# Third batch in groups of 256 rows, with seven half-size products for its second feed-forward product

## The chip, the cores and the metric

The kernel runs on one core of a Trainium2 chip. The metric is the device time of one execution in microseconds (us), and a time given for a kernel is the median of its runs. The engines are TensorE (PE; its weight loads are shown apart as PEld), VectorE (DVE), ScalarE (ACT), GpSimd (POOL) and SyncE (SP, which issues most DMAs).

## What is computed

Two layers, one after the other. The first is a linear attention with a decaying state, over 4 batches, 8 heads, 768 steps and 64 dimensions:

```
state = gamma[h] * state + k_t v_t^T          # per head, 64 x 64
y_t   = q_t @ state / sqrt(64)
```

Its output, as x of 4 x 768 x 512, goes through a Fourier mix and a feed-forward layer:

```
X   = fft(fft(x, axis=1), axis=2)
u   = x + real(X)
un  = (u - mean(u)) / sqrt(var(u) + 1e-6)      # over the 512 columns
out = u + max(un @ w_ch1, 0) @ w_ch2           # w_ch1 512 x 2048, w_ch2 2048 x 512
```

## The kernel before

The kernel works batch by batch (0 to 3). For each batch it runs the attention in four pairs of heads, in chunks of 128 steps; then the Fourier mix, written as matmuls against cosine and sine tables after the input has been folded by its symmetries; then, by blocks of 128 rows, the norm; then the feed-forward layer. Attention and Fourier mix of one batch are interleaved with the feed-forward layer of the batch before, so that TensorE always has matmuls to do.

The order of work is written out by hand as a list of units, in the string `LATER` (its third part, behind the second bar, holds nearly all of it). Every unit issues a few instructions on one to three engines, and `held` pins each instruction behind the one before it on its own engine, so that the list fixes the order on every engine; an engine that waits holds all that stands behind it. Units are named by kind and digits, the first digit being the batch. The names used below:

- `i`, `h`: feed-forward up product of batch 0 by blocks of 128 rows, and of a batch by groups of 384 rows (`h_unit`: 4 matmuls of 384 columns for one of 16 feature blocks, then the relu on ScalarE, `@a`, or VectorE, `@v`). The result lies in the tile `ht16`.
- `c`, `O`: down product (`ch_unit`: for 128 rows, 16 matmuls of 512 columns, four in a unit) and `rows_out`, which scales it, adds u and stores the rows.
- `H`, `j`, `p`, `q`, `w`: the same layer in groups of 256 rows, which batch 3 already uses. `hp_unit` does feature blocks n and n + 8 for 256 rows (8 matmuls of 256 columns; `@s` is two relus on ScalarE, `@b` one on each engine). The down product of a group is then a 2 x 2 block product (features in two halves, output columns in two halves, rows in two blocks of 128), done with seven products instead of eight: `sum_unit` (`j`) forms sums and differences of blocks of the relu's result on VectorE, `wsum_unit` (`w`) those of the weights, `p_unit` does one of seven products (8 matmuls of 256 columns), and `add_unit` (`q`) adds a product to u or to an output row.
- `s`, `a`, `y`: attention (state, masked scores, output; the copy of `y` into x is on ScalarE). `cq`, `ck`, `cv`: casts on GpSimd of the loaded q, k and v; `lq`, `lk`, `lv`, `l`: the loads; `t`, `tq`, `tk`: transposes on TensorE or by DMA.
- `fs`, `fd`, `fe`, `g`: folds of x on VectorE; `f`: first transform; `gr`: mirrored copies; `x`: second transform; `X`: GpSimd adds x to u; `n`, `u`: statistics and normalised rows; `U`: their transpose (`@d` by DMA).

What is loaded lands in a pool of input tiles (`inp`, eleven buffers), which rotate. Down products, up products and the seven products share three PSUM buffers (`ps_pm`).

Of the kernel before, what the change touches and what calls it, by code (L numbers as in the profile page):

```python
# [12 lines left out]
ALU = mybir.AluOpType  # L13
f32 = mybir.dt.float32
# [5 lines left out]
P = 128  # L20
B, H, S, D = 4, 8, 768, 64
DM = 512
# [30 lines left out]
i02 U01@v x03 U02@a cq11 pz11 i12 x04 X03 x05 i13 X04 l10 n03 i10 l11 l12 i22 i11 cq10 i20 X05  # L53
ck10 l13 i23 n04 i03 i21 u04 n05 c0000 c0001 c0002 cv10 u05 u03 Z r00 ck11 c0003 TB cv11 t10
cq12 c0020 c0021 s100 s101 O00 t11 c0022 cv12 a102 U05@a c0023 a100 ck12 a101 s110 s111 a110
c0010 U03@a c0011 a112 a111 y100 c0012 U04@v s120 y101 y110 cq13 ck13 t12 cv13 s121 c0013 pz00
h014@a y111 t13 O02 O01 h012@a h01F@a pz01 a120 a122 h018@a a121 h01D@a a132 a130 a131 s130 s131
h01E@a y120 lq20 y121 h013@a h01C@a lk20 h015@a lv20 lq21 y130 lk21 y131 ck21 fs10 fd10 h01B@a
h010@a h011@a cq20 h019@a lv21 lq22 fs11 ck20 fd11 lk22 lv22 lq23 g10 tq20 h016@a fe10 h017@a
tk20 fe11 c0100 h01A@v f100@v f110@a lk23 f101@v gr11@v tk21 f111@a c0120 g112 x11 X11 x10 r01  # L60
X10 n11 gr13@v x12 X12 c0101 pz10 cv21 n10 u10 gr10@a c0121 u11 c0102 c0103 c0110 c0111 gr12@v
c0112 cq21 c0113 tq21 O03 c0122 lv23 ck22 n12 u12 O04 U12@v cv20 lq30 s210 U11@a U10@v a202 cv22
c0123 s211 x13 h10E@a r10 tk22 a200 a201 h101@a h105@a s200 cq22 h106@a s201 h102@a ck23 a212
h10F@a O05 a210 s220 h10A@v y200 y201 tq22 cv23 X13 tk23 cq23 h100@a a211 x14 X14 s221 h104@v
h103@a y210 y211 tq23 h10C@a lk30 n14 n13 s230 lv30 h107@a x15 X15 h108@a h10B@a h109@a c1000
a220 c1001 c1002 lq31 cq30 n15 u13 a221 a231 a222 ck30 s231 u15 U15@d a230 u14 U14@d h10D@a tk30
c1010 a232 y221 y220 fs20 c1003 U13@d lk31 c1011 lv31 O10 fd20 y230 y231 fs21 g20 c1020 c1012
c1021 c1022 h116@a c1023 c1013 fd21 cq31 fe20 f200@a fe21 tq30 O12 h112@v lq32 lk32 lv32 f210@v
lq33 h111@a cv31 cv30 h11F@a gr20@a f201@v h118@v gr21@a f211@v g212 h115@a h113@a O11 a302
h11E@v x20 h114@v x22 ck31 X20 tq31 h110@a s300 s301 X22 n20 tk31 ck32 gr23@v x21 X21 h11C@a  # L70
h11B@a lk33 cv32 lv33 h119@a h11A@a s310 h117@a s311 n21 c1110 n22 c1100 c1101 c1102 h11D@a
c1111 gr22@v u22 x23 a300 U22@d a301 u20 U20@d a311 x25 c1112 c1103 X25 ck33 a310 u21 r11 a312
c1113 U21@d O14 c1120 cq33 O13 y300 w11 cq32 c1121 c1122 c1123 O15 h20A@v w21 x24 h200@a h20E@v
y301 X23 h20D@v tq32 h209@v h207@a h20C@v tk32 cv33 r20 tk33 h201@v n23 s330 h20F@a s331 y310
y311 s320 h20B@a h208@v u23 h202@a s321 X24 n24 h203@v h206@a h204@v a320 a322 u24 h205@a tq33
c2010 c2020 a321 c2021 U23@d a330 y320 U24@d y321 n25 a331 u25 c2011 U25@d a332 c2022 c2012 y330
fs30 c2023 fd30 c2013 O21 O22 y331 fs31 g30 fd31 fe31 c2000 h210@a c2001 c2002 h21A@a h217@v
c2003 fe30 h21C@a f311@v h21B@v O20 h212@v f300@v f310@a h218@a gr30@v f301@a gr31@a h213@a
h219@a g312 h216@v x31 x30 X30 h214@a h211@v r21 h21F@a h21D@v x32 h215@v X31 c2100 h21E@a c2120
n31 c2101 c2102 w41 u31 U31@d c2110 n30 w10 w20 w40 u30 U30@d gr32@v c2121 c2122 c2123 O25 c2103  # L80
c2111 O23 w31 H304@v c2112 c2113 O24 gr33@a X32 x33 X33 H300@s w30 n32 H302@a H303@a H301@a
j30104 j30204 u32 H305@b j30304 n33 H306@s H307@b j30148 j30248 U32@d r30 j30404 p301 q301 p304
p305 q305 j30448 j30348 u33 U33@d p302 q302 p306 q306 x35 X35 p303 p307 H313@s q307 n35 q303 x34
H317@b H312@s H310@a H314@v H311@b j31104 j31204 u35 U35@d X34 H316@s n34 H315@s j31148 p311
p314 j31248 j31448 p315 r31 q311 q315 p312 j31404 p316 j31304 q316 j31348 u34 U34@d q312 p313
q313 p317 q317 H325@v H320@v H326@a H323@b H324@a j32136 j32336 H321@v H322@b H327@s j32236
j32103 j32168 p321 p324 j32203 p322 j32368 j32268 r32 q321 j32436 j32303 q322 p326 p325 j32403
q326 p327 q325 j32468 p323 q327 q323
# [7 lines left out]
def kernel(  # L96
# [13 lines left out]
    def pool(name, bufs, **kw):  # L110
# [3 lines left out]
    inp = pool("inp", 11)  # L114
# [12 lines left out]
    obp = pool("obp", 3)  # L127
# [21 lines left out]
        "p (n w) -> p n w", n=4)  # L149
    pmask = const.tile([P, 4], f32, tag="pmask")  # L150
# [64 lines left out]
    def in_tile(name, b):  # L215
        return inp.tile([P, 2, NCH, D], f32, tag="in32", name=f"{name}32")
# [4 lines left out]
    def load_unit(b, i, after=None, names="qkv"):  # L221
        def run():
            h0 = 2 * PAIR_ORDER[i]
            for name in names:
# [3 lines left out]
                t = in_tile(name, b)  # L228
# [12 lines left out]
    def first_load(name, i, eng):  # L241
        def run():
            h0 = 2 * ORD0[i]
            t = in_of[name, 0, i] = in_tile(name, 0)
# [887 lines left out]

# [274 lines left out]
```

## Time and profile before

| | us |
|---|---|
| median of 3 runs | 241.01 (240.26 to 241.2) |
| the profiled execution | 240.78 |
| its span, first to last instruction | 238.4 |
| TensorE busy | 225.2 (94%) |
| VectorE busy | 193.1 (81%) |
| ScalarE busy | 125.0 (52%) |
| GpSimd busy | 83.8 (35%) |

The mean granted clock of TensorE is 0.997 of its full speed. Busy time is the share of the span in which an engine has an instruction in it; matmuls are pipelined, and their ends are modelled, so the time that one costs is read from the distance to the start of the next. In rows of the timeline the columns are start, time, engine, source line, operation, tiles, shapes and count, and in brackets the idle time before and what ended it. In rows of groups the columns behind the count are busy time, mean of one in ns, and idle time before with what ended it. In rows of stretches they are the stretch, then busy time (and number of instructions) of TensorE, its weight loads, VectorE, ScalarE and GpSimd, then granted clock, DMA share and GB/s.

### The profile page before, as it was taken

To read this page: it belongs to the slowest core of one execution; us is meant where nothing else is said; L and a number is where in the kernel's file an instruction comes from. 1 tells how busy PE (TensorE), PEld (TensorE's weight loads), DVE (VectorE), ACT (ScalarE), POOL (GpSimd) and SP (SyncE) were. 2 spreads that over 40 slices of the span, in tenths; PEclk is the share of its full clock that TensorE was granted. 3 is DMA by queue.
4 is the path that set the end of the run, shared out by engine and by line. 5 is a ranking of instruction groups with operands and counts; after the bars stand their busy time and mean duration, and the time that the engine had idled before them with its cause. 6 is when DMAs were issued, how large, how long until landed. Compare 5 with 4: busy or idle time off the path is not lost.

```text
span 238.4 us, 5552 instructions
## 1 busy us (share of the span) xinstructions
PE 225.2 (94%) x2135; PEld 155.6 (65%) x2135; DVE 193.1 (81%) x459; ACT 125.0 (52%) x284; POOL 83.8 (35%) x148
## 2 busy tenths in 40 slices
PE   0888999999999999999999999999999999999993
PEld 0366769856776746766576565655576468898893
DVE  8799984978879798988978879877968768869584
ACT  5989759386788345584245253533245307153220
POOL 8378902554600697553144529200005002120000
PEclk9999999999999999999999999999999999999998
DMA  7999999999999999999799983840210222122202
GB/s 169 237 268 238 234 206 207 207 247 264 196 236 204 224 198 210 218 225 219 157 251 215 213 120 133 160 85 22 88 47 0 44 91 67 25 88 45 91 0 88
DMA packets 101225, 37.18 MB, mean 156 GB/s; under 512 B 91472, under 2 KB 98256, under 8 KB 101200
## 3 DMA queue, kind: packets, MB, share of 16 engines
q1 hardware_dynamic: 96976, 32.65, 66.3%
q0 software_dynamic: 4224, 4.19, 10.7%
q8 instruction: 16, 0.26, 0.5%
q14 instruction: 9, 0.07, 0.1%
HBM read 27.66 MB, written 6.29 MB: 142 GB/s over the span
## 4 chain that ended last, share of the span: by engine, by line
PE 78%; DVE 8%; ACT 5%; DMA 3%; POOL 2%; SPq 1%; issue 1%; DVEq 0%; ACTq 0%
PE psc L1129 24%; PE psh L1094 21%; PE psh L1165 9%; PE ps L1216 7%; PE wkA L678 3%; DMA v<-in_v_dram 3%; PE ps L850 3%; PE wkY L721 2%; PE pq L1004 2%; PE wkY L718 1%; DVE ht L1084 1%; PE wkK L697 1%; ACT qTz L649 1%; SPq L246 1%; PE ps L831 1%
## 5 line engine op out<-in xcount | busy, mean ns | idle before, releaser
L1129 PE MATMUL psc<-w,ht 128*128 128x512 f16 x288 | 67.7, 379 | 0.0
L1087 ACT ACTIVATE ht<-psh 128x384 f16<-128x384 f32 (+2 forms) x89 | 41.7, 481 | 42.5 <-PE psh L1094 25.0
L1094 PE MATMUL psh<-unT,w 128*128 128x384 f16 x320 | 59.7, 326 | 0.1
L1129 PEld LDWEIGHTS <-ht 128*128 128x128 f16 x288 | 27.4, 98 | 27.4
L1037 POOL TENSOR_TENSOR u<-u,x 128x256 f32<-128x256 f32 x21 | 13.4, 636 | 81.9 <-DVE u L1011 71.2
L1094 PEld LDWEIGHTS <-w 128*128 128x128 f16 x320 | 29.9, 98 | 17.1 <-issue 0.3
L1084 DVE TENSOR_SCALAR ht<-psh 128x384 f16<-128x384 f32 (+2 forms) x40 | 22.5, 568 | 6.3 <-ACT ht L1087 2.3
L680 DVE TENSOR_TENSOR atm<-wkA,maskp 128x512 f16<-128x512 f32 x36 | 23.3, 682 | 4.9 <-PE wkA L678 4.8
L466 POOL TENSOR_SCALAR kd<-k,gexp 128x384 f16<-128x384 f32 x24 | 13.9, 592 | 23.4 <-DMA k<-in_k_dram 20.8
L1165 PE MATMUL psh<-unT,w 128*128 128x256 f16 x192 | 21.8, 273 | 0.0
L1165 PEld LDWEIGHTS <-w 128*128 128x128 f16 x192 | 18.7, 98 | 2.3
L1053 ACT ACTIVATE un<-u,stats 128x512 f16<-128x512 f32 x21 | 14.8, 718 | 8.9 <-DVE stats L1049 8.2
L728 ACT ACTIVATE x<-wkY,gexp 128x384 f16<-128x384 f32 x24 | 13.0, 585 | 12.1 <-PE wkY L721 12.1
L704 DVE SCALAR_TENSOR_TENSOR s<-s,gk,wkK 128x128 f16<-128x128 f16 x48 | 16.5, 345 | 3.5 <-ACT s L702 1.8
L1119 DVE SCALAR_TENSOR_TENSOR ob<-psc,stats,u 128x512 f32<-128x512 f32 x18 | 13.1, 739 | 5.0 <-PE psc L1129 4.9
L1006 ACT COPY qn<-pq 128x128 f32<-128x128 f32 x18 | 5.1, 283 | 19.8 <-PE pq L1004 17.0
L1216 PEld LDWEIGHTS <-ht 128*128 128x128 f16 x152 | 14.1, 98 | 1.8 <-ACT ht L1087 0.2
L475 POOL TENSOR_SCALAR v<-v 128x768 f16<-128x768 f32 x12 | 10.0, 840 | 13.0 <-DMA v<-in_v_dram 13.0
L1048 DVE BATCH_NORM_STATS2 bst<-u 128x6 f32<-128x512 f32 x21 | 14.3, 681 | 0.1
L1039 POOL TENSOR_TENSOR u<-u,x 128x256 f32<-128x256 f32 x21 | 14.2, 678 | 0.0
L678 PE MATMUL wkA<-qTz,kT 128*128 128x256 f16 x72 | 11.7, 272 | 0.0
L1107 PE MATMUL psh<-unT,w 128*128 128x128 f16 x192 | 11.6, 219 | 0.1
(190 smaller groups left out, 389.4 us busy)
## 6 DMA issues: line engine op xcount, KB each, us to landing
q<-in_q_dram SPq DMA_DIRECT2D x17, 384.0 KB, 6.2
k<-in_k_dram SPq DMA_DIRECT2D x16, 384.0 KB, 5.6
v<-in_v_dram SPq DMA_DIRECT2D x16, 384.0 KB, 6.5
out_dram<-ob SPq DMA_DIRECT2D x23, 256.0 KB, 2.6
w<-in_moe_w_ch_dram POOLq DMA_DIRECT2D x8, 512.0 KB, 11.4
unT<-un SPq DMA_TRANSPOSE x15, 2.5
kT<-kd SPq DMA_TRANSPOSE x10, 3.1
qTz<-q16z SPq DMA_TRANSPOSE x8, 3.9
```

Source lines behind the costliest of these rows:

```text
L678: nc.tensor.matmul(wk[:, c2], st["kT"][:, c, :], st["qT"][:, :, c, :], start=True, stop=True)
L680: nc.vector.tensor_tensor(out=st["atm"][:, 2 * part:2 * part + 2], in0=wk, in1=maskp[:, PAIR_ORDER[i]].unsqueeze(1).to_broadcast([P, 2, 2, ...
L704: nc.vector.scalar_tensor_tensor(out=s16[:, c], in0=s16[:, c - 1], scalar=gk2[:, hp:hp + 1], in1=wk[:, c - c0], op0=ALU.mult, op1=ALU.add)
L1039: nc.gpsimd.tensor_tensor(out=u[:, kb, 256:512], in0=u[:, kb, 256:512], in1=x[:, kb, 1, 257:1:-1], op=ALU.add)
L1048: nc.vector.bn_stats(bst, u[:, kb, :])
L1053: nc.scalar.activation(un, u[:, kb, :], AF.Identity, bias=stats[:, kb, 0:1], scale=-1.0)
L1084: nc.vector.tensor_scalar(out=dst, in0=src, scalar1=-1.0, scalar2=0.0, op0=ALU.mult, op1=ALU.max)
L1087: nc.scalar.activation(dst, src, AF.Relu, bias=0.0, scale=-1.0)
L1094: nc.tensor.matmul(psh, w116[:, cb, fb * P:(fb + 1) * P], unT[:, cb, rt * 384:(rt + 1) * 384], start=(cb == 0), stop=(cb == 3))
L1129: nc.tensor.matmul(psc_of[b, rb], ht16[:, fb, rb3 * P:(rb3 + 1) * P], w216[:, fb, :], start=(fb == 0), stop=(fb == NFB - 1))
L1165: nc.tensor.matmul(psh[:, t], w116[:, cb, fb * P:(fb + 1) * P], unT[:, cb, g * 256:(g + 1) * 256], start=(cb == 0), stop=(cb == 3))
L1216: nc.tensor.matmul(dst, lhsT, rhs[:, c0:c1], start=(n == 0 and (name is not None or k == 5 and m == 1)), stop=(n == 7), skip_group_check=True)
```

## The change

Batch 2 now does its feed-forward layer as batch 3 does: three groups of 256 rows, each with eight `H` units, twelve `j` units (each sum in three parts: feature blocks 0 to 3, 4 to 6 and 7), seven `p` and six `q` units, in place of 32 `h`, 24 `c` and six `O` units. Its `rstd` units go by two blocks instead of three.

The weights' sums are therefore needed a batch sooner, at a time when all input tiles are in use. So their places are fixed: the first sum lies in the tables `cd16` and `sd16`, which nothing reads after the half tables are made; the other three lie in a new constant tile `wide` of the size of four input tiles. Until batch 2's loads are used up, `wide` serves as four of the eleven input buffers (a load whose turn modulo eleven is 7 or more goes there), and the pool itself shrinks from eleven buffers to seven, which are all that batch 3's loads have. The fourth sum of the relu's result gets a tile `s4` of its own. The pool of output rows shrinks from three buffers to two. A unit `C` (`cg_unit`) is added that the list doesn't use.

The third part of `LATER` is a new list, from batch 0's last units on: other engines for some relus and copies, other places for loads and attention, and another order of the last products (it ends with `p326 q322 q325 j32468 p323 q326 p327 q323 q327`, where it was `q322 p326 p325 j32403 q326 p327 q325 j32468 p323 q327 q323`). The diff, with the middle of the list cut to its part for batch 2:

```diff
@@ the list, new (part) @@
+i02 U01@v i03 x03 X03 U02@a x04 X04 i10 i13 i11 l10 x05 X05 i12 cq10 c0010 n04 i22 l11 c0011
...
+u22 c1113 O14 c1122 a312 w40 c1123 U22@d a311 X25 O15 n25 H202@s s300 ck33 s301 H204@s H203@a
+u23 a300 s311 H201@a a310 H200@a j20104 H207@a j20178 y300 w31 H205@s y301 w30 tk32 j20204
+j20404 cq33 H206@s j20147 j20347 r20 j20378 y310 U23@d tk33 j20278 y311 p201 p204 lv33 cv33 tq32
+q201 j20247 j20304 j20447 tq33 p202 q202 p206 p205 q206 p207 u25 n24 q205 u24 j20478 q207 s320
+s330 r21 s321 H217@a j21178 a320 p203 q203 j21278 U24@d a322 a321 a331 H213@s H210@s s331 j21478
+H212@a H211@a j21104 j21304 j21204 j21378 a332 H215@a H214@s j21404 H216@a a330 y321 j21147
+j21347 p211 j21247 q211 j21447 y320 fs30 y331 y330 p214 p216 fs31 q216 fd31 p215 q215 U25@d p217
+g30 fd30 fe30 fe31 p212 p213 q212 f300@a f301@a q217 f310@v f311@a q213 H221@a g312 x31 gr30@v
+X31 x30 X30 n31 n30 H226@a H222@s H223@a H220@a j22104 j22204 u31 x32 H224@b H225@s H227@b r22
...
@@ pools @@
-    inp = pool("inp", 11)
+    inp = pool("inp", 7)
...
-    obp = pool("obp", 3)
+    obp = pool("obp", 2)
...
+    s4t = const.tile([P, 8, P], f16, tag="s4")
@@ input tiles @@
-    def in_tile(name, b):
+    wide = const.tile([P, 4, 2, NCH, D], f32, tag="wide")
+    early = [(n, 0, i) for n, i in LOADS0] + [("q", 1, 0), ("q", 1, 1)]
+    turns = early + [x for b in (1, 2) for i in range(4) for x in [(n, b, i) for n in "qkv"]
+                     if x not in early]
+
+    def in_tile(name, b, i):
+        n = turns.index((name, b, i)) % 11 if b < 3 else 0
+        if n >= 7:
+            return wide[:, n - 7]
         return inp.tile([P, 2, NCH, D], f32, tag="in32", name=f"{name}32")
@@ sums of weights @@
-    def spare(n, name):
-        t = inp.tile([P, 2, NCH, D], f32, tag="in32", name=name)
-        return t.rearrange("p h c d -> p (h c d)").bitcast(f16)[:, 0:n]
+    tw = wide.rearrange("p s h c d -> p (s h c d)").bitcast(f16).rearrange(
+        "p (k n m) -> p k n m", k=3, n=8)
+
+    def t_of(k, part):
+        if k == 1:
+            return (cd16, sd16)[part].rearrange("p a b -> p (a b)").rearrange(
+                "p (n m) -> p n m", n=4)
+        return tw[:, k - 2, 4 * part:4 * part + 4]
...
-            t = seven["t", k, part] = spare(4 * 256, "wsum").rearrange("p (n m) -> p n m", n=4)
...
-            in1 = half_of(w216, *b, n0, n1) if b else seven["t", k // 2, part]
-            nc.vector.tensor_tensor(out=t, in0=half_of(w216, *a, n0, n1), in1=in1,
+            in1 = half_of(w216, *b, n0, n1) if b else t_of(k // 2, part)
+            nc.vector.tensor_tensor(out=t_of(k, part), in0=half_of(w216, *a, n0, n1), in1=in1,
                                     op=ALU.subtract)
...
@@ units @@
-    ... r=lambda b, g: rstd_unit(b, g, 3 if b < B - 1 else 2), c=ch_unit,
+    ... r=lambda b, g: rstd_unit(b, g, 3 if b < 2 else 2), c=ch_unit, C=cg_unit,
```

More of the change, by code (lines that the diff above doesn't have):

```diff
@@ L52 @@
 |
[L53 to L64, printed above, removed]
@@ L71 @@
[L71 to L82, printed above, removed]
@@ new lines @@
+c0012 n05 TB Z u04 i21 c0013 u05 U05@a r00 n03 c0000 c0001 l12 l13 ck10 t10 cv10 i23 ck11 pz01
+c0002 s100 s101 c0003 cq11 O00 a101 cq12 u03 O01 cv11 i20 U03@a a100 t11 c0020 a102 ck12 U04@v
+cv12 c0021 s110 c0022 s111 y100 y101 h015@v t12 pz00 a111 cq13 a110 h013@a lq20 a112 s120 h011@a
+s121 h01B@v h012@v ck13 cv13 s130 s131 y110 y111 t13 lk20 lv20 lq21 c0023 a120 a122 h01E@a
+h010@a a121 a132 ck20 h018@a a131 y121 y120 O02 pz10 a130 h014@a lk21 lv21 h01C@a h016@a y131
+fs10 lq22 lk22 lv22 y130 fs11 fd10 r01 h01D@a fd11 h01A@a tk20 h017@a h019@a c0100 c0101 cq20
@@ L89 @@
+p322 j32336 p324 p325 q321 j32268 p326 q322 q325 j32468 p323 q326 p327 q323 q327
 """
@@ L1131, in ch_unit, with cg_unit, run @@
         return run
+    def cg_unit(b, g, t, part):
+        def run():
+            rb = 2 * g + t
+            if part == 0:
+                psc_of[b, rb] = ps_pm.tile([P, DM], f32, tag="pm", name="psc")
+            for fb in range(4 * part, 4 * part + 4):
+                nc.tensor.matmul(psc_of[b, rb], hg[:, fb % 8, fb // 8, t * P:(t + 1) * P],
+                                 w216[:, fb, :], start=(fb == 0), stop=(fb == NFB - 1))
+        return run
     seven = {}
@@ L1176, in run @@
         def run():
-            if "s4" not in seven:
-                seven["s4"] = spare(8 * P, "s4").rearrange("p (n k) -> p n k", n=8)
             a11, a12 = hg[:, n0:n1, 0, 0:P], hg[:, n0:n1, 1, 0:P]
@@ L1341 @@
     later = dict(
[L1342 removed]
+        pz=pad_unit,         i=h0_unit, r=lambda b, g: rstd_unit(b, g, 3 if b < 2 else 2), c=ch_unit, C=cg_unit,
         O=lambda b, rb: lambda: rows_out(b, rb), X=add_x_unit, cq=cq_unit, ck=ck_unit,
```

44 lines of the change are left out of this document (26 added, 18 removed).

## The prediction

> **What bounds the kernel now.** I read the page first (busy time, then the chain that ended last), then the busy time of each engine by stretches, then TensorE's own timeline, where the pitch of a matmul is the distance from one row's start to the next row's start.
>
> ```profile
> PE 225.2 (94%) x2135; PEld 155.6 (65%) x2135; DVE 193.1 (81%) x459; ACT 125.0 (52%) x284; POOL 83.8 (35%) x148
> PE 78%; DVE 8%; ACT 5%; DMA 3%; POOL 2%; SPq 1%; issue 1%; DVEq 0%; ACTq 0%
> ```
>
> ```profile
> 40.00:60.00 20.00, 19.20 (x218) 14.02 (x216) 17.43 (x46) 12.74 (x22) 10.41 (x16) 1.00 1.17 236
> 60.00:80.00 20.00, 19.90 (x221) 14.05 (x218) 17.41 (x39) 14.70 (x30) 4.77 (x9) 1.00 1.10 213
> 80.00:100.00 20.00, 20.00 (x174) 12.60 (x173) 17.19 (x44) 10.29 (x29) 14.64 (x26) 1.00 1.21 220
> 146.60:192.75 46.15, 46.15 (x358) 27.62 (x356) 36.80 (x81) 19.43 (x44) 7.28 (x12) 1.00 0.27 63
> ```
>
> TensorE is the bound: it carries 78% of the chain, and from 80 us (the third row) to the tail every stretch of 20 us shows it busy throughout. The fourth row is the stretch that the change rewrites, from the last down product of batch 1 to the first unit of batch 3's feed-forward: TensorE 46.15 of 46.15 us at clock 1.00, VectorE 36.80 (80%), ScalarE 42%. The first two rows hold the only waits worth naming, 0.8 and 0.1 us. So the time of this kernel is the sum of its matmuls plus the places where a list of units leaves TensorE waiting, and I price the change in these two terms.
>
> **The matmuls.** Pitches come from these rows.
>
> ```profile
> 179.99 2.76 PE L1094 MATMUL psh<-unT,w 128*128 128x384 f16 x16
> 182.59 0.39 PE L1004 MATMUL pq<-gk,g 128*128 128x129 f16 x4
> 184.98 7.93 PE L1129 MATMUL psc<-w,ht 128*128 128x512 f16 x36
> 192.75 1.04 PE L1165 MATMUL psh<-unT,w 128*128 128x256 f16 x8
> 202.57 1.91 PE L1216 MATMUL ps<-wsum,ht 128*128 128x256 f16 x16
> 204.32 1.04 PE L1216 MATMUL ps<-w,ht 128*128 128x256 f16 x8
> ```
>
> 384 columns: 2.60 us / 16 = 162.5 ns. 512 columns: 7.77 / 36 = 215.8 ns. 256 columns: 1.75 / 16 = 109.4 ns. Batch 2 now has 2 x 16 x 4 = 128 up matmuls of 384 columns (20.80 us) and 6 x 16 = 96 down matmuls of 512 (20.72). After, it has 3 x 8 x 8 = 192 up matmuls of 256 (21.00) and 3 x 7 x 8 = 168 down products of 256 (18.38). Sum: 39.38 for 41.52, so **-2.1 us**. Everything else on TensorE keeps its count.
>
> The Trainium skill would have this otherwise. "TensorE: Matmul & The Clock Gate", section "Back-to-back issue gap", says that in a stream of weight loads and matmuls the spacing is set by both, and gives about 81 ns at 128 moving columns and 131 at 512; drawn straight between them (an estimate from that page) 384 columns cost 114 and 256 cost 98, and the change would add 35.3 - 27.2 = 8.1 us. The three pitches above do not agree with those figures, and the measurement decides; the mechanism returns as a rival.
>
> **VectorE.** These groups carry its new work.
>
> ```profile
> L1185 DVE TENSOR_TENSOR ht<-ht 128x512 f16<-128x512 f16 x12 | 5.0, 420 | 1.3 <-ACT ht L1087 1.1
> L1185 DVE TENSOR_TENSOR ht<-ht 128x384 f16<-128x384 f16 x6 | 2.0, 353 | 0.7 <-ACT ht L1087 0.7
> L1230 DVE SCALAR_TENSOR_TENSOR u<-ps,stats,u 128x256 f32<-128x256 f32 x6 | 2.9, 483 | 0.5 <-PE ps L1216 0.3
> L1230 DVE SCALAR_TENSOR_TENSOR ob<-ps,stats,u 128x512 f32<-128x512 f32 x3 | 2.3, 751 | 0.7 <-PE ps L1216 0.6
> L1119 DVE SCALAR_TENSOR_TENSOR ob<-psc,stats,u x18: 630/746/752, 55.5 to 195.6; 128x512 f32<-128x512 f32 x18
> L1084 DVE TENSOR_SCALAR ht<-psh 128x384 f16<-128x384 f32 x23 | 12.6, 552 | 1.9 <-PE psh L1094 1.6
> L1153 DVE TENSOR_TENSOR wsum<-w x4: 674/680/954, 144.6 to 197.1; 128x1024 f16<-128x1024 f16 x4
> ```
>
> Added: 36 sums, a third each of four, three and one blocks (420, 353, and some 200 ns for one block, which no row shows: bounds 100 and 353), 12 x 0.97 = 11.7 us; 18 adds, 12 x 0.483 + 6 x 0.751 = 10.3. Gone: 6 row adds of 0.746 (4.4) and the 16 relus that VectorE did for h2 (16 x 0.552 = 8.8), since the new H2 units carry @a or @s (ScalarE) but for two @b. Six weight sums lay in the quoted stretch and four of them leave it (-2.9; 0.7 us each between 100 and 145 us, behind batch 1's products; by the third row VectorE has 14% free thereabouts, so I cost them at nothing; without that cover 8 x 0.7). Some 3 us more of batch 3's attention now fall into it. At full means the old stretch sums to 42.3 us, of which 36.80 are busy time, since successive instructions overlap: a factor of 0.87. The new one sums to 50.8, so 44 us busy for about 47.7 us of matmuls. VectorE goes from 80% to 92%: not the bound, but without room to catch up. ScalarE, 42% busy in the old stretch, takes over the relus with room left.
>
> **The place where that shows** is the fold of batch 3, where the old order has rows for each step:
>
> ```profile
> 167.12 0.34 PE L721 MATMUL wkY<-v,atm 128*128 128x64 f16 x6
> 167.50 0.58 ACT L728 ACTIVATE x<-wkY,gexp 128x384 f16<-128x384 f32 x1 [1.47 <-PE wkY L721]
> 168.50 1.02 DVE L747 TENSOR_TENSOR xab<-x 128x768 f16<-128x768 f16 x2
> 169.56 0.17 DVE L874 TENSOR_TENSOR xg<-xab 128x6 f16<-128x6 f16 x1
> 169.90 1.02 DVE L774 TENSOR_TENSOR eo<-xab 128x768 f16<-128x768 f16 x2
> 170.96 0.57 DVE L788 TENSOR_TENSOR ee<-eo 128x768 f16<-128x768 f16 x1
> 172.51 0.56 DVE L788 TENSOR_TENSOR ee<-eo 128x768 f16<-128x768 f16 x1
> 173.57 0.18 DVE L793 COPY ee<-eo 128x6 f16<-128x6 f16 x1
> ```
>
> By starts, fs costs 1.06 us, g30 0.34, fd 1.06, and fe30 with its copy 1.24. The old list had all of c200x and a dozen h21x as filler. The new one reads y320 fs30 y331 y330 p214 p216 fs31 q216 fd31 p215 q215 p217 g30 fd30 fe30 fe31 p212 p213 ... f300. Count from the moment T at which TensorE has issued y330. TensorE then has six products before f300: 6 x 8 x 0.1094 = 5.25 us. VectorE starts fs30 at about T + 0.3, after y320's copy and the last sums, and ends it at T + 1.35; the copy of y330, last of three at some 0.5 each, is done by T + 1.1. Then fs31 1.06, q216 0.48, fd31 1.06, q215 0.75, g30 0.34, fd30 1.06, fe30 1.24: 6.0 us, so f300 may start at T + 7.3, or some tenths sooner with overlap. TensorE waits for 7.3 - 5.25 = 2.1; with 0.2 for the overlap I take **+1.9 us** (bounds 1.6 and 2.6, the latter if VectorE comes late). q216, q215 and g30 stand in that queue without being needed there. Afterwards f310 finds fe31 done within 0.1 us, H221 and g312 cover the copies, and the first H30 unit stands 22 us behind y330 while its chain (product, add, statistics, norm, transpose) needs some 20: nothing more.
>
> **Early waits.** The new list differs from batch 1's first units on.
>
> ```profile
> 52.73 0.50 PE L644 MATMUL tq<-ident,q16z 128*128 128x128 f16 x6
> 53.95 0.51 PE L644 MATMUL tq<-ident,kd 128*128 128x128 f16 x6 [0.73 <-ACT s L702]
> 54.30 1.03 PE L1129 MATMUL psc<-w,ht 128*128 128x512 f16 x4
> 52.64 1.26 POOL L466 TENSOR_SCALAR kd<-k,gexp 128x384 f16<-128x384 f32 x2 [2.77 <-DMA k<-in_k_dram]
> 63.66 0.83 POOL L475 TENSOR_SCALAR v<-v 128x768 f16<-128x768 f32 x1
> out_dram<-ob SPq DMA_DIRECT2D x23, 256.0 KB, 2.6
> ```
>
> t11 waited there until GpSimd's ck11 had ended at 53.9 (the label names ScalarE; the time fits ck11): its first half took 1.22 us from row to row, the second 0.35, so 0.9 was lost. In the new list t11 stands 19.5 us of matmuls behind i02 instead of 16.8, and the loads, which start behind i13, come 0.45 later: that wait goes, **-0.9**. In turn s130 moves up from 31.7 to 28.6, which is 64.5 on this clock (i02 being at 52.73 - 16.8 = 35.9), while cv13 ended at 64.49 and now ends 0.45 later: **+0.4**. The smaller pool of input tiles costs nothing: for batches 0 to 2 the rotation over eleven is the same, and batch 3's twelve loads find casts that ended well before. The two output buffers (three before) come free 2.6 us after a store is issued, and the next is needed later than that each time.
>
> **The end.** Rows of the old end:
>
> ```profile
> 233.93 1.01 DVE L1230 SCALAR_TENSOR_TENSOR ob<-ps,stats,u 128x512 f32<-128x512 f32 x2 [0.25 <-PE ps L1216]
> 234.17 0.61 PE L1216 MATMUL ps7e<-w,s 128*128 128x128 f16 x8
> 235.13 0.88 SPq L1262 DMA_DIRECT2D out_dram<-ob  x2
> DMA to landing us min/median/max: 1.7/1.8/1.9
> DMA to landing us min/median/max: 2.0/2.0/3.0
> ```
>
> It ended with p323, whose row leaves in two small stores; the second is issued at 235.6 and lands 1.7 later, 2.7 after the last matmul was issued (234.6). The new list ends with p327: 0.2 to the add, 0.75 for it, then the full store with 2.0: 3.0, so **+0.3**. Waits of the new list that I did not find: 0 to 1.5, by the 0.9 of the old one's worst 40 us; I take 0.2.
>
> **Sum:** -2.1 + 1.9 - 0.9 + 0.4 + 0.3 + 0.2 = -0.2 us on the profiled execution's own 240.78 (span 238.4), which stands 0.2 below the median of 241.01. Against that median: **240.8 us**. I treat 0.5% (1.2 us) as what a measurement of this kernel can tell from no change.
>
> **Rivals.**
> *The fold is covered.* If VectorE is ahead of my count, or its steps overlap more, f300 finds its data; then -2.1 stands nearly alone: about 238.6. For it: the old list left TensorE no wait over 0.3 us after 80 us, by an order just as tight. Against: the six products are 5.25 us, and even with nothing in between, fs31, fd31, fd30 and fe30 are 4.4 us behind a copy that ends at T + 1.1. 0.28.
> *VectorE becomes the bound,* from the first H2 unit to the first H3 unit. Price: its 50.8 us at full means, without the overlap, plus some 2 us of waits for GpSimd's additions, would be 52.8 for 47.7 of matmuls: 5.1 us in place of the fold's 1.9, about 244.0. It decides once VectorE's idle share there falls below some 5%. For it: 92% already. Against: the factor of 0.87 in the old stretch. 0.20.
> *The shared read port.* L1153's rows run from 674 to 954 ns: something holds a two-input VectorE instruction for 0.28 us at times. If that is GpSimd, the added sums and the weight sums, now among GpSimd's casts, meet it more often: five meetings in the full stretch are 1.4 us, about 242.2. The Trainium skill, "SBUF — State Buffer", section "Who interferes with whom", has this rule: VectorE with two SBUF inputs and GpSimd exclude each other for a whole instruction. Other two-input rows (L774, 546 to 559) did not show it. 0.06.
> *Weight loads show.* There are 136 more pairs of load and matmul; if a load of 98 ns were not hidden, +13.3 us: 252. The 109.4 ns pitch with a load in each speaks against it. 0.01.
> *The change does not do what it says:* the order is pinned on every engine, so this would be sums or buffers put elsewhere, with the time as it was: 0.03.
>
> ```profile
> L774 DVE TENSOR_TENSOR eo<-xab x12: 546/552/559, 72.9 to 170.4; 128x768 f16<-128x768 f16 x12
> L1216 PEld LDWEIGHTS <-ht 128*128 128x128 f16 x152 | 14.1, 98 | 1.8 <-ACT ht L1087 0.2
> ```
>
> **How the numbers follow.** My forecast has 0.42, with a range of its own from 239.6 to 242.0. Faster by over 0.5%: the covered fold and a little of the forecast's edge, 0.31. Slower: VectorE's bound, the port, the loads and the other edge, 0.31. Within: 0.38. The range takes in the covered fold and stops short of the middle of VectorE's case: 238.5 to 243.2.
>
> **What would show it.** TensorE's rows of batch 2: 192 + 168 matmuls of 256 columns at 109 ns. A gap of about 2 us in TensorE ahead of f300 (L850 of batch 3), ended by VectorE's fold (L790 or L793). No wait ahead of t11's second half, a short one ahead of s130. VectorE at 90 to 94% between H202 and H300. No gap at f300, or several of them at sums and adds, would prove me wrong.

## Result and profile after

The changed kernel takes **237.68 us** (median of 4 runs, 237.33 to 238.87) beside 241.1 for the kernel before (4 runs, 240.26 to 241.88): a ratio of 0.987, interval 0.982 to 0.992. Taken a second time with more runs of the kernel before, it was 237.46 (5 runs) for 240.32, ratio 0.988 [0.986, 0.990]. It is faster by some 3 us, where the prediction had 240.8 and a range from 238.5 to 243.2. The profiled execution took 237.73 us, its span 235.7.

The page of the changed kernel, the engines' busy time and the chain:

```profile
PE 223.2 (95%) x2271; PEld 168.9 (72%) x2271; DVE 197.0 (84%) x490; ACT 133.3 (57%) x304; POOL 83.6 (35%) x148
PE 84%; DVE 5%; SPq 5%; DMA 3%; POOL 1%; issue 1%; ACT 0%; POOLq 0%; DVEq 0%
```

TensorE is still the bound, with 84% of the chain for 78%, and its busy time is 2.0 us less. Next the stretches. The first three rows are the changed kernel's (the prediction's stretch; the same units where they now lie, from H202 to H300; the early part), the fourth is the kernel before in the stretch of the third, the fifth is the changed kernel's just ahead of f300:

```profile
146.60:192.75 46.15, 45.46 (x506) 40.86 (x505) 42.57 (x116) 25.43 (x61) 6.72 (x11) 1.00 0.37 80
144.00:191.60 47.60, 46.91 (x519) 42.13 (x517) 43.84 (x119) 26.93 (x65) 6.81 (x11) 1.00 0.42 84
33.00:60.00 27.00, 27.00 (x341) 21.14 (x339) 21.70 (x56) 18.81 (x39) 12.80 (x19) 1.00 1.18 225
```

```profile
33.00:60.00 27.00, 26.06 (x316) 20.02 (x314) 21.31 (x55) 18.28 (x38) 10.41 (x16) 1.00 1.19 229
```

```profile
164.60:175.10 10.50, 9.82 (x122) 8.66 (x120) 10.22 (x26) 3.85 (x8) 0.00 (x0) 1.00 0.05 11
```

VectorE is busy for 42.57 of 46.15 us, 92% (43.84 of 47.60 where the units now lie, also 92%), and in the last 10 us ahead of f300 for 97%; TensorE loses 0.69 us there. From 33 to 60 us TensorE had idled 0.94 us and now does not idle at all.

The matmuls of batch 2, from TensorE's timeline of the changed kernel (24 up matmuls, then p214 and p216, then the row that follows):

```profile
163.99 2.78 PE L1193 MATMUL psh<-unT,w 128*128 128x256 f16 x24
166.61 0.38 PE L689 MATMUL wkA<-qTz,kT 128*128 128x256 f16 x2
...
168.98 1.91 PE L1242 MATMUL ps<-wide,ht 128*128 128x256 f16 x16
170.73 0.60 PE L1242 MATMUL ps<-cd,ht 128*128 128x256 f16 x4
```

2.62 us / 24 and 1.75 / 16 are 109 ns each, with a weight load for every one.

The place of the forecast, f300. First VectorE's timeline of the changed kernel from fs30 on, then TensorE's (p217, p212, p213, f300):

```profile
169.22 1.97 DVE L758 TENSOR_TENSOR xab<-x 128x780 f16<-128x780 f16 x4
171.11 0.48 DVE L1256 SCALAR_TENSOR_TENSOR u<-ps,stats,u 128x256 f32<-128x256 f32 x1
171.51 1.01 DVE L785 TENSOR_TENSOR eo<-xab 128x768 f16<-128x768 f16 x2
172.44 0.74 DVE L1256 SCALAR_TENSOR_TENSOR u<-ps,stats,u 128x512 f32<-128x512 f32 x1
173.10 0.16 DVE L885 TENSOR_TENSOR xg<-xab 128x6 f16<-128x6 f16 x1
173.30 0.23 DVE L888 TENSOR_SCALAR xg<-xg,sgn 128x6 f16<-128x6 f16 x1
173.43 1.02 DVE L785 TENSOR_TENSOR eo<-xab 128x768 f16<-128x768 f16 x2
174.49 0.57 DVE L799 TENSOR_TENSOR ee<-eo 128x768 f16<-128x768 f16 x1
```

```profile
171.64 1.03 PE L1242 MATMUL ps<-wide,ht 128*128 128x256 f16 x8
172.51 1.04 PE L1242 MATMUL ps<-w,ht 128*128 128x256 f16 x8
173.39 1.04 PE L1242 MATMUL ps<-w,s4t 128*128 128x256 f16 x8
175.11 1.38 PE L861 MATMUL ps<-csp,ee 128*128 128x193 f16 x12 [0.69 <-DVE ee L799]
```

p213 starts at 173.39, and eight matmuls at 109 ns end at 174.26; f300 starts at 175.11. So it waits 0.85 (the 0.69 in the bracket counts from the modelled end), released by the first of fe30's three instructions, L799. Another 0.16 stands ahead of f301.

The early part, from TensorE's timeline: the kernel before, batch 0's up product and the row that follows; then the changed kernel: up units in the same place, t11 (both halves and what follows) and, in the last two rows, an up unit and s130; then GpSimd's cv13 in the changed kernel.

```profile
39.14 7.62 PE L1107 MATMUL psh<-unT,w 128*128 128x128 f16 x128
46.60 3.62 PE L1129 MATMUL psc<-w,ht 128*128 128x512 f16 x16
```

```profile
40.70 0.38 PE L1031 MATMUL pq<-cd,g16r 128*128 128x257 f16 x2
...
41.13 1.06 PE L1118 MATMUL psh<-unT,w 128*128 128x128 f16 x16
42.03 1.03 PE L1140 MATMUL psc<-w,ht 128*128 128x512 f16 x4
...
54.34 0.50 PE L655 MATMUL tq<-ident,q16z 128*128 128x128 f16 x6
54.68 0.50 PE L655 MATMUL tq<-ident,kd 128*128 128x128 f16 x6
55.01 1.03 PE L1140 MATMUL psc<-w,ht 128*128 128x512 f16 x4
...
62.38 1.46 PE L1105 MATMUL psh<-unT,w 128*128 128x384 f16 x8
63.67 0.44 PE L708 MATMUL wkK<-v,kd 128*128 128x128 f16 x5
```

```profile
62.23 0.83 POOL L486 TENSOR_SCALAR v<-v 128x768 f16<-128x768 f32 x1
```

The old list ran 128 up matmuls in one go, 7.46 us from start to start; at the 56 ns of the new list (0.90 / 16) they would have taken 7.2. The rest is two waits inside the run, 0.08 us at 41.9 and 0.24 at 44.8. Two more stand ahead of it, 0.27 at 37.07 (a transpose that waits for ScalarE's `un`) and 0.07 at 39.14. The new list has these up matmuls in shorter runs between other units, most of them sixteens, and all four waits are gone; one of 0.16 at 36.03 has come in. Both halves of t11 now take their plain 0.34 us. s130 (63.67) stands behind the end of cv13 (63.06, where the old list had 64.49), so it waits for nothing; a small wait of 0.19 us is ahead of an up unit at 62.38 instead.

The end: the last product (p327), its add and its store in the changed kernel's timeline, with the landing times of the group of that store's line.

```profile
230.66 1.04 PE L1242 MATMUL ps<-wide,ht 128*128 128x256 f16 x8
...
231.74 0.75 DVE L1256 SCALAR_TENSOR_TENSOR ob<-ps,stats,u 128x512 f32<-128x512 f32 x1 [0.52 <-PE ps L1242]
232.52 0.33 SPq L1282 DMA_DIRECT2D out_dram<-ob  x1
```

```profile
DMA to landing us min/median/max: 2.0/2.0/2.5
```

The store lands at 234.5, 3.0 us behind the last matmul's issue at 231.5; before it was 2.7.

Put together (waits are taken from TensorE's timeline as the distance between starts less the pitch of the form; the bracketed idle times are shorter, since ends are modelled):

| term | forecast, us | measured, us |
|---|---|---|
| matmuls of batch 2 | -2.1 | -2.1 |
| f300 and f301 | +1.9 | +1.0 |
| t11 | -0.9 | -0.9 |
| other waits, 33 to 60 us | 0 | -0.7 |
| s130, and waits from 60 to 150 us | +0.4 | -0.1 |
| first 33 us | 0 | -0.4 |
| tail (measured to the end of the span) | +0.3 | +0.4 |
| waits not found | +0.2 | +0.1 |
| sum | -0.2 | -2.7 |

The span went from 238.4 to 235.7, which is that sum.

### The profile page after: what moved, and what is told of

Same layout as the page of the kernel before. It is cut to its first block, busy times and chain, and to the rows that moved or that the text cites. A ratio compares the mean times of both kernels' runs of the same rounds, so it can differ in the third digit from the quotient of the medians.

```text
span 235.7 us, 5892 instructions
## 1 busy us (share of the span) xinstructions
PE 223.2 (95%) x2271; PEld 168.9 (72%) x2271; DVE 197.0 (84%) x490; ACT 133.3 (57%) x304; POOL 83.6 (35%) x148
## 4 chain that ended last, share of the span: by engine, by line
PE 84%; DVE 5%; SPq 5%; DMA 3%; POOL 1%; issue 1%; ACT 0%; POOLq 0%; DVEq 0%
PE psh L1193 18%; PE psc L1140 18%; PE psh L1105 13%; PE ps L1242 13%; PE psh L1118 5%; SPq L257 5%; PE wkA L689 3%; PE ps L861 3%; DMA wide<-in_q_dram 3%; PE pq L1015 2%; PE wkY L732 1%; PE wkK L708 1%; PE wkY L729 1%; PE ps L842 1%; PE tq L655 1%; DVE xab L758 1%
## 5 line engine op out<-in xcount | busy, mean ns | idle before, releaser
L1098 ACT ACTIVATE ht<-psh 128x384 f16<-128x384 f32 (+2 forms) x106 | 49.0, 480 | 44.4 <-PE psh L1193 28.5
L1140 PE MATMUL psc<-w,ht 128*128 128x512 f16 x192 | 45.8, 379 | 0.0
L1193 PE MATMUL psh<-unT,w 128*128 128x256 f16 x384 | 44.6, 273 | 0.0
L1193 PEld LDWEIGHTS <-w 128*128 128x128 f16 x384 | 37.1, 98 | 4.1
L1048 POOL TENSOR_TENSOR u<-u,x 128x256 f32<-128x256 f32 x21 | 13.3, 635 | 64.2 <-DVE u L1022 53.0
L1105 PE MATMUL psh<-unT,w 128*128 128x384 f16 x192 | 34.8, 326 | 0.0
L1242 PEld LDWEIGHTS <-ht 128*128 128x128 f16 x296 | 27.8, 98 | 3.4 <-ACT ht L1098 0.2
L1140 PEld LDWEIGHTS <-ht 128*128 128x128 f16 x192 | 18.0, 98 | 16.8
L1105 PEld LDWEIGHTS <-w 128*128 128x128 f16 x192 | 18.2, 98 | 10.6 <-issue 0.2
L1211 DVE TENSOR_TENSOR ht<-ht 128x512 f16<-128x512 f16 (+3 forms) x48 | 15.9, 352 | 7.5 <-ACT ht L1098 7.1
L1095 DVE TENSOR_SCALAR ht<-psh 128x512 f16<-128x512 f32 (+2 forms) x24 | 13.4, 567 | 6.2 <-ACT ht L1098 3.4
L1242 PE MATMUL ps<-wide,ht 128*128 128x256 f16 x144 | 18.5, 273 | 0.0
L1050 POOL TENSOR_TENSOR u<-u,x 128x256 f32<-128x256 f32 x21 | 13.3, 635 | 0.0
L1242 PE MATMUL ps<-w,ht 128*128 128x256 f16 x96 | 12.4, 273 | 0.0
L1118 PEld LDWEIGHTS <-w 128*128 128x128 f16 x192 | 11.4, 98 | 1.2 <-issue 0.3
```

Of the source, the lines that this page charges most:

```text
L1098: nc.scalar.activation(dst, src, AF.Relu, bias=0.0, scale=-1.0)
L1105: nc.tensor.matmul(psh, w116[:, cb, fb * P:(fb + 1) * P], unT[:, cb, rt * 384:(rt + 1) * 384], start=(cb == 0), stop=(cb == 3))
L1118: mm = nc.tensor.matmul(psh[:, f], w116[:, cb, fb * P:(fb + 1) * P], unT[:, cb, kb * P:(kb + 1) * P], start=(cb == 0), stop=(cb == 3))
L1140: nc.tensor.matmul(psc_of[b, rb], ht16[:, fb, rb3 * P:(rb3 + 1) * P], w216[:, fb, :], start=(fb == 0), stop=(fb == NFB - 1))
L1193: nc.tensor.matmul(psh[:, t], w116[:, cb, fb * P:(fb + 1) * P], unT[:, cb, g * 256:(g + 1) * 256], start=(cb == 0), stop=(cb == 3))
L1211: nc.vector.tensor_tensor(out=out_, in0=x, in1=y, op=op)
```

## Experiments

### The new places without the new list

The changed kernel's tiles (`wide`, seven input buffers, two output buffers, `s4`) with the old list of units.

```diff
-i02 U01@v i03 x03 X03 U02@a x04 ...      (new third part of LATER)
+i02 U01@v x03 U02@a cq11 pz11 i12 ...    (old third part)
-    r=lambda b, g: rstd_unit(b, g, 3 if b < 2 else 2)
+    r=lambda b, g: rstd_unit(b, g, 3 if b < B - 1 else 2)
```

> The changed kernel's tiles (constant tile wide, seven input buffers, two output buffers, fixed places for the weight sums) with the old list. Theory (the time is TensorE's matmuls plus its waits, and the tiles cost nothing): within 0.4 us of the kernel before, TensorE's waits as in it, 1.7 us between 33 and 60 us of the span. Rival (the tiles themselves move the time, by loads that wait or come sooner): 0.6 us or more away, with waits at other places.

240.86 us (10 runs) for 240.58, ratio 1.000 [0.997, 1.002]. TensorE's waits from 33 to 60 us are 1.6 us, as in the kernel before with 1.7. The smaller pools cost nothing that shows within the interval's 0.6 us, and give nothing: the gain is in the list.

### The early order alone, both ways

First the kernel before with the new order up to unit h01E, and the old order of what is left behind it; then the changed kernel with the old order up to h01E.

```diff
-i02 U01@v x03 U02@a cq11 pz11 i12 ... s130 s131 h01E@a
+i02 U01@v i03 x03 X03 U02@a x04 ... a120 a122 h01E@a   (then the old order)
```

> The kernel before with the new list's order as far as batch 1's last attention pair (up to its unit h01E), then the old order. Theory (the early waits went with the new order there, apart from the seven products): 1.2 to 1.6 us faster than before, no wait of 0.9 us ahead of t11's second half, 0.2 us ahead of h015 or s130. Rival (the early gain comes from something else in the changed kernel): as before, within 0.4 us.

```diff
-i02 U01@v i03 x03 X03 U02@a x04 ... a120 a122 h01E@a
+i02 U01@v x03 U02@a cq11 pz11 i12 ... s130 s131 h01E@a   (then the new order)
```

> The changed kernel with the old list's order up to the unit h01E, then the new order. Theory: the early waits come back, 1.2 to 1.6 us slower than the changed kernel, so 1.8 to 2.2 faster than before, the wait at f300 as in it (about 1.0 us). Rival: as the changed kernel, within 0.4 us.

The first took 241.29 us for 240.58, ratio 1.003 [1.002, 1.005], where 1.2 to 1.6 us less was expected. t11's wait went, but its timeline has this in its stead, a down unit that waits for a transfer of weights:

```profile
46.98 1.02 PE L1128 MATMUL psc<-w,ht 128*128 128x512 f16 x4 [0.66 <-DMA w<-in_moe_w_ch_dram]
```

and 2.2 us of waits lie where the two orders meet, from 60 to 80 us. As a splice it can't say what the new order is worth.

The second took 239.89 us, ratio 0.998 [0.996, 1.000]: 2.2 to 2.4 us slower than the changed kernel, more than the 1.2 to 1.6 expected. All waits of 33 to 60 us that the old list had came back, at the same units: 0.27, 0.07, 0.08 and 0.24 us between 36.8 and 44.6, and t11, which the row itself names:

```profile
53.78 0.51 PE L654 MATMUL tq<-ident,kd 128*128 128x128 f16 x6 [0.45 <-POOL kd L476]
```

1.47 us from 33 to 60 us in place of 0.16, and 1.0 more from 60 to 150, of which 0.6 is at f100 behind the seam. The wait at f300 was as before, 0.85. So the early part of the new list takes away about 1.3 us of waits from 33 to 60 us by itself, and not only at t11; the rest of the 2.2 to 2.4 lies at the seam and in the first 33 us, and the splice can't say how much of it is the order's.

### Eight products in batch 2

Batch 2's down product done plainly, 96 matmuls of 512 columns, without sums and with row adds; all else is the changed kernel.

```diff
-p201 p204 ... q201 ... p203 q203      (7 products, 6 adds, 12 sums of each group)
+C2000 C2001 ... O20 ... C2013 O21     (16 matmuls of 512 columns for each 128 rows)
```

> The changed kernel with batch 2's down product done plainly in the same groups of 256 rows: 96 matmuls of 512 columns (the unit C) for 168 of 256, six row adds for 18 adds, no sums in batch 2. The weight sums stay, since batch 3 uses them. Theory (seven products pay by their matmuls, and VectorE's added work costs the 1.0 us at f300): matmuls +2.3 us, the wait at f300 shorter by 0.8 to 1.0, so 1.3 to 1.5 us slower than the changed kernel and 1.7 to 2.1 faster than before. Rival (the order of the new list makes the whole gain): as the changed kernel, within 0.4 us. Rival (VectorE bounds the stretch): faster than the changed kernel.

238.9 us (4 runs) for 240.58, ratio 0.994 [0.992, 0.995]. The last matmul starts 1.2 us later than in the changed kernel. Its timeline at f300:

```profile
171.66 4.05 PE L1148 MATMUL psc<-w,ht 128*128 128x512 f16 x18
175.55 1.34 PE L858 MATMUL ps<-csp,ee 128*128 128x193 f16 x12
```

18 x 0.216 = 3.89, so f300 follows without a wait (0.14 in all). The seven products bring 2.3 us of matmuls and give 0.9 back at f300: a net gain of 1.2 to 1.4, in the trace and in the time.

### The fold's start moved ahead

The first theory of f300's wait was latency: y330's product, its copy and the folds behind it. Here y320, y331 and y330 stand ahead of p211, and fs30 ahead of q211. The changed kernel itself was measured beside it.

```diff
-a332 H215@a H214@s j21404 H216@a a330 y321 j21147 j21347 p211 j21247 q211 j21447 y320 fs30 y331 y330 p214 p216 fs31
+a332 a330 H215@a H214@s j21404 H216@a y321 y320 y331 y330 j21147 j21347 p211 j21247 fs30 q211 j21447 p214 p216 fs31
```

> The changed kernel once more, as the measure for the three beside it. Every theory: as in its first runs, 3.0 to 3.4 us faster than before, 1.0 us of wait at f300 and f301.

> The changed kernel with one product more behind y330: a330 moves up behind a332, y320 y331 y330 ahead of p211, and fs30 ahead of q211. Nothing is added or taken away. Theory (f300 waits for VectorE's chain that starts with y330's copy; the six products behind y330 are too few): the wait at f300 and f301 falls from 1.0 us to 0.0 to 0.3, and the time by 0.7 to 1.0 us against the changed kernel. Rival (VectorE is the bound over the whole stretch): the wait turns up again behind f300, at the next sums or adds, and the time stays within 0.3 us of the changed kernel.

237.48 us for the unchanged kernel's 237.46: ratios 0.988 [0.986, 0.990] both. VectorE's fs30 and TensorE's f300 in its timeline:

```profile
168.66 1.04 DVE L757 TENSOR_TENSOR xab<-x 128x780 f16<-128x780 f16 x2
```

```profile
175.23 1.37 PE L860 MATMUL ps<-csp,ee 128*128 128x193 f16 x12 [0.55 <-DVE ee L798]
```

fs30 starts 0.56 earlier, and f300 does not. p216 now waits 0.3 and f300 0.72. The latency of y330 is not what holds f300; VectorE has next to no idle time from 164.6 us on that could be won.

A further kernel (`best`) was to join this edit with the next one and put g30 behind fe31; it gave no time, because its order cannot run. g30 behind fe31 locks it up: the tile `ee`, which fe30 writes, takes the one buffer that `xab` lies in, g30 still has to read `xab`, and VectorE comes to g30 only behind fe31. So g30 can't be moved out of the way on VectorE; the last experiment puts it on another engine.

### The last products with p327 ahead, as in the old order

```diff
-p326 q322 q325 j32468 p323 q326 p327 q323 q327
+p326 q322 q325 j32468 q326 p327 p323 q327 q323
```

> The changed kernel with the end in the old order: p327 ahead of p323, so that the last thing to leave is a store of 128 columns and not one of a full row. Theory (the last store's landing sets the end): the last landing is 2.7 us behind the last matmul instead of 3.0, 0.3 us faster than the changed kernel. Rival (the end is set by other work): no change, within 0.1 us by the trace.

238.27 us for 240.32, ratio 0.991 [0.988, 0.993], against an expected gain of 0.3. By the ratios it is about 0.6 us slower than the changed kernel, though the intervals overlap; by the trace it is 0.3. The last store is back at 2.7 us behind the last matmul, but p327 has a wait of its own:

```profile
230.28 1.03 PE L1241 MATMUL ps<-wide,ht 128*128 128x256 f16 x8 [0.58 <-DVE u L1255]
```

It adds to the sums that q326 has to read first, and p323 no longer fills that time. The new tail costs 0.4 at the store and saves 0.7 ahead of it.

### Where VectorE is the bound

Three relus moved to VectorE in the first group of batch 2, and three in the second.

```diff
-H203@a ... H201@a ... H207@a        -H217@a ... H212@a ... H215@a
+H203@v ... H201@v ... H207@v        +H217@v ... H212@v ... H215@v
```

> The changed kernel with three relus of batch 3's group 0 (units H203, H201, H207 of batch 2's first group of 256 rows) moved from ScalarE to VectorE: some 2.0 us more of VectorE work, issued between 146 and 152 us, ahead of the stretch 164.6 to 175.1 us in which VectorE is busy without a gap. Theory (VectorE sets the time only in that gapless stretch, and catches up before it): the time of the changed kernel, 237.5, plus 0 to 0.4, the wait at f300 still 0.8 to 1.1. Rival A (VectorE is the bound of the whole stretch from H202 to H300, as the prediction's second rival had it): plus 1.5 to 2.0, about 239.3. Rival B (VectorE is nowhere the bound, f300 waits for the latency of y330's chain): plus 0.

> The changed kernel with three relus of batch 2's second group (H217, H212, H215) moved from ScalarE to VectorE: the same 2.0 us of VectorE work, two of the three units inside or right ahead of the gapless stretch 164.6 to 175.1 us. Theory (VectorE's queue sets when f300 may start): f300's wait grows by 1.2 to 2.0 and the time with it, to 238.7 to 239.5. Rival A (the bound is VectorE over the whole stretch): the same 239.3, and then the first group's relus cost as much. Rival B (latency of y330's chain): plus 0 to 0.3.

First group: 238.29 us for 240.65, ratio 0.989 [0.987, 0.992]. f300's wait is 0.85 as ever, but a new one of 0.95 stands ahead of p206. VectorE's small sums beside GpSimd's cast, and p206 on TensorE:

```profile
153.95 0.97 DVE L1210 TENSOR_TENSOR ht<-ht 128x128 f16<-128x128 f16 x2
```

```profile
153.88 0.83 POOL L485 TENSOR_SCALAR v<-v 128x768 f16<-128x768 f32 x1 [5.85 <-DMA v<-in_v_dram]
```

```profile
155.37 1.03 PE L1241 MATMUL ps<-wide,ht 128*128 128x256 f16 x8 [0.78 <-DVE u L1255]
```

Two sums of one block took 0.97 us (0.34 in the changed kernel): the first took 0.84 instead of 0.2 and ended 0.08 behind GpSimd's cast. q201 stood behind it, and p206 behind q201. So 0.63 of the 0.95 is this meeting, for which the expectation of 0 to 0.4 had no place; some 0.3 of the 2 us added is left as a wait, and the rest was absorbed. The whole stretch is not bound by VectorE.

Second group: 238.86 us, ratio 0.992 [0.989, 0.995], 0.0037 above the changed kernel's 0.9881, some 0.9 us. p217 and f300 on TensorE:

```profile
173.43 1.03 PE L1241 MATMUL ps<-wide,ht 128*128 128x256 f16 x8 [0.58 <-DVE u L1255]
...
176.90 1.29 PE L860 MATMUL ps<-csp,ee 128*128 128x193 f16 x11 [0.69 <-DVE ee L798]
```

1.3 us of new waits (0.50 at p211, 0.13, and 0.74 in place of 0.04 at p217), for 2.0 us of work added. So VectorE does set the time in this second group; but the bracket ahead of f300 is 0.69 again, to the hundredth. What comes late on VectorE is paid at p217, not at f300, where the expectation had it. That made the second theory: q216 must have read its sums before p217 adds to them (both use the first half of one PSUM tile), so every delay is taken out there, and from there on a fixed race runs. VectorE does fd31 0.93, q215 0.66, g30 0.33, fd30 1.06 and the first of fe30 0.62 from row to row, 4.00 from q216's start and 3.47 from p217's; TensorE does three products, 2.62. The rest is 0.85. The starts agree: in all nine profiled runs with this order of units from q216 on, f300 starts 3.99 to 4.01 us behind q216. In eight of them the wait is 0.85; with the fold's start moved ahead it is 0.72, since there p216's wait, and not q216, had already put p217 0.13 later.

(The profiled execution of this kernel, 239.78 us, also has a wait of 0.92 us at 36.45, for a transfer of weights, where the changed kernel has 0.16; the other five took 238.8 to 238.9.)

### The fourth sum on GpSimd

The three instructions of j214 on GpSimd; in the second kernel s130 and s131 stand behind y111 as well.

```diff
-            nc.vector.tensor_tensor(out=out_, in0=x, in1=y, op=op)
+            (nc.gpsimd if (b, g, m) == (2, 1, 4) else nc.vector).tensor_tensor(
+                out=out_, in0=x, in1=y, op=op)
```

> The changed kernel with the fourth sum of batch 2's second group (three instructions, 0.21, 0.42 and 0.35 us on VectorE) on GpSimd, which has nothing to do from 155 to 175 us. Theory (VectorE's queue from 164.6 us to f300): 0.6 to 0.8 us leave the queue, the wait at f300 and f301 falls from 1.0 to 0.2 to 0.5, and the time is 0.4 to 0.8 below 237.5, about 236.9. Rival B (y330's latency): no change, 237.5. Rival C (the shared read port): GpSimd's sums hold VectorE's two-input instructions up for as long as they take, VectorE's rows beside them are longer by 0.5 us or more in sum, and the time is at 237.5 or above.

> As the kernel with the fourth sum on GpSimd, and s130 s131 moved behind y111, so that they stand behind cv13's end: takes away the wait of 0.19 us ahead of s130 as well. Theory: 0.2 us below the kernel with the fourth sum on GpSimd, about 236.7, unless the moved units make another wait: y110 y111 ahead of them need scores that may come 0.1 to 0.3 late, which would give 0.

237.84 and 237.82 us for 240.65, ratios 0.988 [0.985, 0.991] both: no gain, as rival C had it. f300's wait stayed at 0.85 and p217's grew to 0.38. The group of the folds' first step, and GpSimd's last sum:

```profile
L757 DVE TENSOR_TENSOR xab<-x x12: 545/557/966, 70.9 to 170.7; 128x780 f16<-128x780 f16 x6, 128x768 f16<-128x768 f16 x6
```

```profile
168.53 0.91 POOL L1210 TENSOR_TENSOR s4t<-ht 128x384 f16<-128x384 f16 x1 [1.67 <-DVE ht L1210]
```

One fold instruction took 966 ns for 557: it started at 168.90, inside GpSimd's sum. What left VectorE's queue came back as 0.41 us of being held up, and as VectorE's own wait of 0.47 for a330's scores, which one of the sums had covered. Moving s130 took nothing away either: the wait of 0.2 us at 62 us stayed where it was, ahead of an up unit, so it had not been s130's.

### g30 on GpSimd

```diff
+            e = nc.gpsimd if b == B - 1 else nc.vector
-            nc.vector.tensor_tensor(out=xg[:, :, 0:2], in0=src,
+            e.tensor_tensor(out=xg[:, :, 0:2], in0=src,
...
-        nc.vector.tensor_scalar(out=xg[:, :, 2:4], in0=xg[:, :, 0:2], scalar1=sgn, scalar2=None,
+        e.tensor_scalar(out=xg[:, :, 2:4], in0=xg[:, :, 0:2], scalar1=sgn, scalar2=None,
```

> The changed kernel with batch 3's g30 (two instructions on 128x6, 0.33 us from row to row on VectorE) on GpSimd, which is idle there. Six runs of the changed kernel and its variants show one and the same 0.85 us ahead of f300, whatever came before. Theory (a race that starts where q216 frees p217's sums: VectorE then does fd31, q215, g30, fd30 and the first fe30 in 3.47 us, TensorE three products in 2.62): 0.33 leaves VectorE's side, the wait at f300 falls from 0.85 to 0.5 to 0.6, and the time by 0.25 to 0.35, to a ratio of about 0.987 against the kernel before. Rival A (f300 waits for something else, y330's chain or a transfer): 0.85 as before and no change. Rival B (GpSimd holds VectorE's two-input instruction up, as its sums and its cast did in two runs for 0.42 and 0.5 us): the fd30 or q215 row beside it is longer by 0.2 to 0.5, and f300's wait stays at 0.7 to 1.0.

237.34 us (4 runs) for 240.48, ratio 0.986 [0.983, 0.989]. VectorE's fd30 and fe30, then f300 on TensorE:

```profile
173.42 1.02 DVE L784 TENSOR_TENSOR eo<-xab 128x768 f16<-128x768 f16 x2
174.54 0.57 DVE L798 TENSOR_TENSOR ee<-eo 128x768 f16<-128x768 f16 x1
```

```profile
175.17 1.38 PE L860 MATMUL ps<-csp,ee 128*128 128x193 f16 x12 [0.43 <-DVE ee L798]
```

The wait fell from 0.85 to 0.59 (0.69 to 0.43 in the brackets). f300 now starts 3.74 us behind q216, not 4.00. Taking work out of the race moved the wait, by nearly what was taken (0.33), where taking more away ahead of it had not: the race from q216 to fe30 is what f300 waits for. It is the fastest median of the study, though its interval and the changed kernel's overlap: 0.3 us is at the edge of what these runs can tell. (The profiled execution, 237.94, also has an early wait of 0.63 us at 36.3, where the changed kernel has 0.16; the other three took 237.34.)

## Why the prediction was wrong

*The matmuls* were right: -2.1 us, at the very pitches of the kernel before. The spacing that the Trainium skill gives for such a stream ("TensorE: Matmul & The Clock Gate", section "Back-to-back issue gap"), by which the prediction estimated that the change would add 8 us, does not hold here: 109 ns at 256 columns with a weight load each. Weight loads did not show.

*VectorE's share* was right, 92% for a forecast of 92% (its terms add up to 51.2 us, not 50.8, which is 44.5 us busy for 44, and 43.8 were measured), and so was "not the bound of the stretch, but without room": in the first group extra work was mostly absorbed, in the second it was not.

*The fold* had the right place, the right releaser and the wrong size. The failed step is the count from T + 0.3 to T + 7.3. T is 168.98; VectorE started fs30 at T + 0.24, and f300 started at T + 6.13. Two terms were too long. fe30 with its copy stood at 1.24, while f300 needs only its first instruction, released 0.62 after the start: TensorE was taken to wait for a whole unit where it waits for one tile's first part. And the units were added by the distances that the old trace showed with other work between: fs30 with fs31 took 1.89 for 2.12, fd31 0.93 for 1.06, q216 0.40 for 0.48, q215 0.66 for 0.75, since instructions that follow each other without a gap overlap by some 0.1 us. I allowed 0.2 for that; it was 0.5. So 1.0 in place of 1.9. Nor was the place where the count starts right: the prediction counted from y330 and fs30, but moving these ahead brought nothing, and the part that counts starts at q216. It also had it that q216, q215 and g30 "stand in that queue without being needed there". All three are: p217 adds to the sums that q216 has to read first, p213 to those that q215 has to read first, and g30 reads the buffer that fe30 overwrites.

*The early waits* were the second failed step, and as large. t11 was right (-0.9). The rest of that stretch was costed at nothing, although the quoted row showed TensorE idle for 0.80 us from 40 to 60 and waits from 33 to 40 were not looked at: the old list had four smaller waits of 0.7 us in sum, at a transpose and in its long run of up units, which the new list breaks up; the changed kernel with the old early order got them back. "Waits of the new list that I did not find" was given only a plus sign. A list that is written anew can also lose waits that nobody has named. s130's +0.4 did not come: cv13 was to end 0.45 later than in the old list and ended 1.4 earlier, 0.6 us ahead of s130.

*The first 33 us* went 0.4 to 0.5 shorter. Behind the same 312 matmuls, batch 0's first up product starts at 32.5 to 32.8 us in the eleven profiled runs with the new early order, and at 33.3 to 33.7 in the three with the old one. The lists are the same up to there. It goes with the order behind, not with the tiles: the new places with the old list have 33.7, the old places with the new early order 32.5. By what way, the loads or something else, stays open.

*The tail* was right: 3.0 us behind the last matmul, for 2.7. With p327 ahead of p323, as in the old order, it would not have been better.

*The rivals.* The covered fold (238.6; 238.9 with all other terms at their forecast) came nearest in time, yet not for its reason: f300 did wait. That is luck: the time came as much from the early waits, which no rival named. VectorE as the bound of the whole stretch fell with the first of the two relu runs. The shared read port was priced at five meetings in the new stretch. The changed kernel shows one there on VectorE, of 0.27 us and behind f300. Over the whole span its VectorE instructions that run 80 ns or more over the median of their kind, all beside GpSimd work, sum to 2.2 us of excess, and those of the kernel before to 2.3. So it explains no difference between the two, but the mechanism is real here: a sum of one block took 839 ns instead of some 200 when it met a GpSimd cast, a fold instruction 966 for 557 when it met a GpSimd sum. The Trainium skill, "SBUF — State Buffer", section "Who interferes with whom", has it that a VectorE instruction with two inputs from SBUF contends with a GpSimd instruction that reads SBUF, and that the shared ports are an exclusive lock. Both rows agree: each VectorE instruction ended only after GpSimd's had. Weight loads that show were priced at 252, where 13.3 us on 240.8 would be 254; the pitch of 109 ns rules them out. That the change does what it says is seen in the matmuls' forms: 360 more of 256 columns, 128 fewer of 384 and 96 fewer of 512.

*The range* failed with the sum: its lower end, 238.5, lies only 0.4 under the covered fold with every other term at its forecast. The fold and the early stretch both came out 0.9 and more to the fast side.

## What to carry to other kernels

When one engine waits for another in a fixed order, find the event that both pass last (here an add that frees the sums of the next product) and count both sides from there to the wait; what lies ahead of that event moves the event, not the wait. Count to the first instruction that releases the waiting one, with distances from rows that follow each other without a gap. And where a whole order is rewritten, list every wait of the old one above a few hundredths, and ask of each whether it stays: the unknown has two signs.

## What the hardware showed unexpectedly

An instruction taken off a busy VectorE and put on an idle GpSimd can cost VectorE as much as it saves: three sums of 0.98 us in all went, and one two-input instruction was held up for 0.41 us, with 0.35 us more TensorE wait in the end. With g30's two tiny ones it was GpSimd that was late: the second took 1.12 us beside VectorE's folds, whose pairs kept their 1.02 us, and nobody waited for it.

Not only VectorE instructions with two inputs are held up: its copy L868 (one input, 128x384 f16), 258 ns in the median, took 527 in the changed kernel at 180.23 us, beside GpSimd's additions to u.

The same wait of 0.85 us ahead of f300, within 0.005, in eight profiled runs, with up to 2 us more and 1 us less VectorE work in front of it, shows how exactly a wait can be set by a short local race.
